# Splitting weights two row chunks at a time, in the memory their float64 words are loaded into

## The chip, the core and the metric

The kernel runs on one core of a Trainium2 chip. The metric is the device time of one execution in microseconds (us). A core has a matrix engine (PE, TensorE), a vector engine (DVE), a scalar engine (ACT), GpSimd (POOL) and a queue engine (SP) that issues this kernel's DMA transfers. Each engine executes its own instructions in program order and waits on semaphores for the others; the on-chip memory has 128 partitions, and the size of an instruction is given by its elements in each partition.

## The reference

Eight batches of 576 tokens go through an attention over 32 packed queries a head and then through a channel mix:

```python
def sm_attn(qq, kk, vv):
    s = scale * np.matmul(qq, kk.transpose(0, 1, 3, 2))
    s = s - np.max(s, axis=-1, keepdims=True)
    a = np.exp(s)
    a = a / (np.sum(a, axis=-1, keepdims=True) + 1e-09)
    return np.matmul(a, vv)
p_packed = sm_attn(p, k, v)
out = sm_attn(q, p_packed, p_packed)
...
x_prev = np.concatenate([np.zeros((B, 1, D), dtype=np.float32), x[:, :-1, :]], axis=1)
xk = mu_k * x + (1.0 - mu_k) * x_prev
xr = mu_r * x + (1.0 - mu_r) * x_prev
k = np.maximum(xk @ w_k, 0.0)
v = k * k @ w_v
r = 1.0 / (1.0 + np.exp(-(xr @ w_r)))
return (r * v).astype(np.float32)
```

q, k, v and p are float32 of 8 batches x 8 heads x 576 (p: 32) x 64; x has 8 x 576 rows of 512. The weights w_r (512 x 512), w_k (512 x 1024) and w_v (1024 x 512) arrive as float64.

## The kernel before

**Blocks.** The 4608 tokens are handled in nine blocks of 512. For each block PE computes the gates (`gates`: xr with w_r, four row tiles of 128 tokens by four chunks of 128 of the sum), the keys (`keys`: xk with w_k, eight column tiles by four chunks) and the values (`values`: the squared keys with w_v, eight chunks by four row tiles). Each product is three matmuls, since both sides are kept as a rounded high part and a low part (`_h` and `_l`): high by high, high by low, low by high. Block 0 lies inside batch 0; block 1 has 64 rows of batch 0 and 448 of batch 1.

**The attention** of a batch runs ahead of the blocks that need it: k is transposed (`transposed_on_pe` for the first two batches, `transposed` on DVE for the rest), `front` makes the scores of the packed queries, the softmax of `weights_of` and the packed values; `back` makes the second scores (line 611), the second softmax on DVE and ACT (lines 635 to 658, in two halves of the batch that interleave) and the output (line 666); `mixed_in` copies it to `xt` (line 688). `mix` then scales and adds (lines 721 on ACT and 725 on DVE), and `split` makes high and low (741 on ACT, 743 on DVE), xr first.

**The weights.** `convert` takes one row chunk of 128 rows and 512 columns at a time: 4 for w_r, 8 for w_k, 8 for w_v, 20 in all. It takes one of four `staged` slots and one of eight `sq` slots, loads the chunk's float64 words as pairs of 32-bit words (512 KB), and when they have landed takes a `tmp` slot for the float32 words m. Line 286 (ACT) makes exponent and high mantissa from the upper words by a scaled copy, lines 288, 290 and 292 (DVE) shift it, set the sign and add the bits of the lower words. Then `sq` and `staged` are given back, line 296 (ACT) rounds m to the high part and line 298 (DVE) subtracts to the low part, both into constant tiles for the whole weight, and the chunk's event is set. `gates` waits for the events of the chunk's w_r, `keys` for w_k, `values` for w_v.

`sq` slots also hold block 0's xr (four, until the gates are done) and the squared keys (eight a block).

**The order** of all engines is made when the program is built, by a planner (`Flow`). Each piece of work is a generator that asks for events, slots or an engine. The planner always takes the piece that could start first by its own clock; where several could start at once, the lower rank goes first. Its costs for an instruction of n elements are in lines 190 to 200, for a load in 205 to 211. A dependent step is ready 0.22 us after the one before it. What it emits is then the fixed order of each engine's queue; the real waits are semaphores. Ranks: batch 0 about 10, the mixing of block 0 11.5, w_r and w_k 13.6 (`RANK_W`), batch 1's loads 14.29, w_v 15.2 (`RANK_V`). The loads of the first two w_r chunks have ranks of their own, `FIRST`, just behind batch 0's loads. Until the gates of block 0 are nearly done, the planner puts small matmuls (`spare`, line 899) where it expects PE to be idle, to keep its clock up; they compute nothing that is used.

Of the kernel before, what the change touches and what calls it, by code (L numbers as in the profile page):

```python
# [8 lines left out]
F32 = mybir.dt.float32  # L9
F32R = mybir.dt.float32r  # L10
U32 = mybir.dt.uint32
AF = mybir.ActivationFunctionType
ALU = mybir.AluOpType
# [150 lines left out]
def attn_pack_channel_mix(ctx: ExitStack, tc: tile.TileContext, q, k, v, p, mu_k, mu_r, w_k, w_v, w_r, out):  # L164
    nc = tc.nc
    B, H, S, D = q.shape
    NP = p.shape[2]
    DM, DF = w_k.shape
    P = 128
# [5 lines left out]
    NC = DM // P  # L175
    NF = DF // P
# [3 lines left out]
    WP = 512  # L180
# [3 lines left out]
    flow = Flow()  # L184


    FIRST = 10.09, 10.29
    RANK_1, RANK_MIX, RANK_W, RANK_V, LOADS_1 = 14.28, 11.5, 13.6, 15.2, 14.29

    def vec(n, after=None):  # L190
        return "vector", 0.07 + 1.04e-3 * n, after, None

    def vec2(n, after=None):
        return "vector", 0.07 + 0.53e-3 * n, after, None

    def act(n, after=None, table=None):
        return "scalar", 0.14 + 0.72e-3 * n, after, table
# [4 lines left out]
    def pe(us, after=None):  # L202
        return "tensor", us, after, None

    def load(dst, src, issue, us):
        yield "queue", issue, None, None
        nc.sync.dma_start(dst, src)  # L207
        begin = max(flow.free.get("dma", 0.0), flow.t + 0.46)
        flow.free["dma"] = begin + us
        flow.free["queue"] = max(flow.free["queue"], begin - 2.0)  # L210
        flow.now.t = begin + us + LANDS
# [6 lines left out]
    def reached():  # L218

        yield None, 0.0, None, None  # L220
# [3 lines left out]
    const = ctx.enter_context(tc.tile_pool(name="const", bufs=1))  # L224
    sb = ctx.enter_context(tc.tile_pool(name="sb", bufs=1))
    ps = ctx.enter_context(tc.tile_pool(name="ps", bufs=1, space=bass.MemoryType.PSUM))
    BUFS = dict(raw=3, kq=4, vt=2, pt=1, a=2, aT=1, pm=2, e=2, a2=1, xt=4, tmp=4, xk=NC, sq=NF, sig=4,
                pa=2, both=1, m=4, staged=4)
    dram = ctx.enter_context(tc.tile_pool(name="dram", bufs=1, space=bass.MemoryType.DRAM))
    for tag, n in BUFS.items():  # L230
        flow.pool(tag, n)
# [2 lines left out]
    def tile_(shape, dtype, tag, slot, name=None):  # L234
        return sb.tile(shape, dtype, name=name or tag, tag=f"{tag}{slot}")
# [22 lines left out]
    ident = const.tile([P, P], F32, name="ident")  # L258
    make_identity(nc, ident)

    wk_h = const.tile([P, NC, DF], F32R, name="wk_h")
    wk_l = const.tile([P, NC, DF], F32R, name="wk_l")
    wr_h = const.tile([P, NC, DM], F32R, name="wr_h")
    wr_l = const.tile([P, NC, DM], F32R, name="wr_l")
    wv_h = const.tile([P, NF, DM], F32R, name="wv_h")
    wv_l = const.tile([P, NF, DM], F32R, name="wv_l")

    def convert(w, hi, lo, c, o, n, event, first=None):

        rank = flow.now.rank  # L270
        if first:
            flow.now.rank = first
        staged = yield from flow.take("staged")
        slot = yield from flow.take("sq")
        st = tile_([P, 2 * WP], U32, "sq", slot, "st")
        yield from load(st[:, :2 * n], w[c * P:(c + 1) * P, o:o + n].bitcast(U32), 0.46, 3.5e-3 * n)
        flow.now.rank = rank
        yield from reached()
        sm = yield from flow.take("tmp")
        m = tile_([P, WP], U32, "tmp", sm, "m")[:, :n]  # L280
        w0, w1 = (st[:, :2 * n].rearrange("p (n two) -> p two n", two=2)[:, j, :] for j in range(2))

        yield act(n)
        nc.scalar.activation(m.bitcast(F32), w1.bitcast(F32), AF.Copy, scale=2.0 ** -112)
        yield vec2(n)
        nc.vector.tensor_scalar(m, m, 3, None, op0=ALU.logical_shift_left)
        yield vec(n, after=0.0)
        nc.vector.scalar_tensor_tensor(m, w1, 0x80000000, m, op0=ALU.bitwise_and, op1=ALU.bitwise_or)  # L290
        yield vec(n, after=0.0)
        nc.vector.scalar_tensor_tensor(m, w0, 29, m, op0=ALU.logical_shift_right, op1=ALU.bitwise_or)
        flow.give("sq", slot)
        flow.give("staged", staged)
        yield act(n)
        nc.scalar.copy(hi[:, c, o:o + n], m.bitcast(F32))
        yield vec(n)
        nc.vector.tensor_tensor(lo[:, c, o:o + n], m.bitcast(F32), hi[:, c, o:o + n].bitcast(F32), op=ALU.subtract)
        flow.give("tmp", sm)
        flow.set(event)  # L300

    ts, vts, pts, xts, xt2 = {}, {}, {}, {}, {}

# [42 lines left out]
    def back_to_issue():  # L346
        flow.now.t = flow.free["queue"]
# [402 lines left out]
    def keys(i):  # L750
        for f in range(NF):
            slot = yield from flow.take("m")
            ph = ps.tile([P, 512], F32, name="ph", tag=f"m{slot}")[:, :TB]
            fs = slice(f * P, (f + 1) * P)
            for c in range(NC):
                yield from flow.wait(("xk", i, c), ("wk", c, f * P // WP * WP))
                yield pe(0.69)
                flow.now.t -= flow.LAG
                _, xh, xl = xks[i, c]
                nc.tensor.matmul(ph, wk_h[:, c, fs], xh, start=(c == 0), stop=False)  # L760
                nc.tensor.matmul(ph, wk_h[:, c, fs], xl, start=False, stop=False)  # L761
                nc.tensor.matmul(ph, wk_l[:, c, fs], xh, start=False, stop=(c == NC - 1))  # L762
                if f == NF - 1:
                    flow.give("xk", xks.pop((i, c))[0])
            flow.spawn(squared(i, f, slot, ph), 0, flow.t + flow.LAG)
# [19 lines left out]
    def gates(i):  # L785
        for t in range(NT):
            slot = yield from flow.take("m")
            pr = ps.tile([P, DM], F32, name="pr", tag=f"m{slot}")
            ts_ = slice(t * P, (t + 1) * P)
            if i == 0 and t == NT - 1:  # L790

                flow.keep_busy = 0.0
                flow.give("m", 3)
            for c in range(NC):
                yield from flow.wait(("xr", i, c), *(("wr", c, o) for o in range(0, DM, WP)))
                yield pe(0.69)
                flow.now.t -= flow.LAG
                _, xh, xl = xrs[i, c]
                nc.tensor.matmul(pr, xh[:, ts_], wr_h[:, c, :], start=(c == 0), stop=False)  # L799
                nc.tensor.matmul(pr, xh[:, ts_], wr_l[:, c, :], start=False, stop=False)  # L800
                nc.tensor.matmul(pr, xl[:, ts_], wr_h[:, c, :], start=False, stop=(c == NC - 1))  # L801
                if t == NT - 1:
                    flow.give("sq", xrs.pop((i, c))[0])
            flow.spawn(gated(i, t, slot, pr), 0, flow.t + flow.LAG)

    def gated(i, t, slot, pr):
        sg = yield from flow.take("sig")
        sig = tile_([P, DM], F32, "sig", sg)
        yield act(DM, table="sigmoid")
        nc.scalar.activation(sig, pr, AF.Sigmoid)  # L810
        flow.give("m", slot)
        sigs[i, t] = sg, sig
        flow.set(("sig", i, t))

    def values(i):
        slots, pv = {}, {}
        for f in range(NF):
            yield from flow.wait(("sq", i, f), *(("wv", f, o) for o in range(0, DM, WP)))
            sf, hl = sqs.pop((i, f))
            for t in range(NT):  # L820
                if f == 0:
                    slots[t] = yield from flow.take("m")
                    pv[t] = ps.tile([P, DM], F32, name="pvo", tag=f"m{slots[t]}")
                ts_ = slice(t * P, (t + 1) * P)
                yield pe(0.69)
                flow.now.t -= flow.LAG
                sh, sl = hl[:, 0, ts_], hl[:, 1, ts_]
                nc.tensor.matmul(pv[t], sh, wv_h[:, f, :], start=(f == 0), stop=False)  # L828
                nc.tensor.matmul(pv[t], sh, wv_l[:, f, :], start=False, stop=False)  # L829
                nc.tensor.matmul(pv[t], sl, wv_h[:, f, :], start=False, stop=(f == NF - 1))  # L830
                if f == NF - 1:
                    flow.spawn(done(i, t, slots[t], pv[t]), 0, flow.t + flow.LAG)
            flow.give("sq", sf)
# [42 lines left out]
        flow.set("mu")  # L876

    def weights():
        first = list(FIRST)
        for c in range(NC):  # L880
            for o in range(0, DM, WP):
                flow.spawn(convert(w_r, wr_h, wr_l, c, o, WP, ("wr", c, o), first.pop(0) if first else None), RANK_W)
        for o in range(0, DF, WP):
            for c in range(NC):
                flow.spawn(convert(w_k, wk_h, wk_l, c, o, WP, ("wk", c, o)), RANK_W)
        for f in range(NF):
            for o in range(0, DM, WP):
                flow.spawn(convert(w_v, wv_h, wv_l, f, o, WP, ("wv", f, o)), RANK_V)

    flow.spawn(all_loads(), 10)  # L890
    flow.spawn(fronts(), 10)
# [36 lines left out]
```

## Time and profile before

| | us |
|---|---|
| median of 3 runs | 599.08 |
| the runs | 602.93, 598.65, 599.08 |
| the profiled execution | 602.04 |
| its span on the core | 600.3 |
| mean granted PE clock (1 is full) | 0.997 |

Two further views are of use. The first is the busy share of each engine in 40 slices of 15 us, in tenths:

```profile
PE   9999999999999999998999999999999999999997
...
DVE  1499999966779769745962977186404812551321
ACT  3578784863585675543833575257524703631410
```

DVE is full from the third slice to the eighth (30 to 120 us), PE nearly everywhere; a slice in which PE computes only fillers reads as busy too. The second is the loads of the weights, issued by SP, with their number, size and the median time from issue to landing:

```profile
st<-in_moe_w_k SPq DMA_DIRECT2D x8, 512.0 KB, 6.2
st<-in_moe_w_v SPq DMA_DIRECT2D x8, 512.0 KB, 5.6
...
st<-in_moe_w_r SPq DMA_DIRECT2D x4, 512.0 KB, 6.7
```

### The profile page before, as it was taken

How to read it: one execution, taken by the hardware profiler on the slowest of the kernel's cores; microseconds unless marked ns; L12 is line 12 of the kernel's file. 1: busy time of each engine (PE TensorE's matmuls, PEld its weight loads, DVE VectorE, ACT ScalarE, POOL GpSimd, SP SyncE). 2: the span in 40 equal slices, each digit the busy share in tenths (PEclk: the TensorE clock that was granted, in tenths of full speed). 3: DMA queues.
4: the chain of work that ended last, by engine and by line, in shares of the span. 5: the costliest groups of instructions: out<-in, count | busy, mean ns of one | idle time of the engine just before them, and what ended most of it. 6: DMA issues, size and time to landing. Idle time of an engine off the chain costs nothing.

```text
span 600.3 us, 10117 instructions
## 1 busy us (share of the span) xinstructions
PE 587.6 (98%) x3924; PEld 465.4 (78%) x3924; DVE 372.3 (62%) x713; ACT 317.4 (53%) x555; POOL 2.1 (0%) x23
## 2 busy tenths in 40 slices
PE   9999999999999999998999999999999999999997
PEld 8777677787777777676777787778788888888886
DVE  1499999966779769745962977186404812551321
ACT  3578784863585675543833575257524703631410
POOL 0000000000000000000000000000000000000000
PEclk9999999999999999998999999999999999999999
DMA  8894661674665760764636343200100010001001
GB/s 194 250 281 120 218 149 42 141 168 84 143 135 130 155 137 15 186 142 70 133 82 166 89 77 93 79 0 1 58 13 1 1 70 1 0 1 70 1 0 71
DMA packets 170895, 56.51 MB, mean 94 GB/s; under 512 B 147808, under 2 KB 162144, under 8 KB 170848
## 3 DMA queue, kind: packets, MB, share of 16 engines
q1 hardware_dynamic: 170848, 55.87, 38.1%
q8 instruction: 31, 0.51, 0.3%
q14 instruction: 16, 0.13, 0.1%
HBM read 42.86 MB, written 12.98 MB: 93 GB/s over the span
## 4 chain that ended last, share of the span: by engine, by line
PE 80%; DVE 6%; SPq 5%; DMA 4%; ACT 2%; issue 2%; ACTq 0%; DVEq 0%
PE pvo L828 11%; PE pvo L830 11%; PE pvo L829 11%; PE ph L760 10%; PE ph L762 9%; PE ph L761 9%; SPq L207 5%; PE pr L799 4%; PE pr L801 4%; PE pr L800 4%; PE pa L666 2%; DVE m L290 2%; PE pa L611 1%; PE pa L478 1%; DMA vt<-in_v 1%
## 5 line engine op out<-in xcount | busy, mean ns | idle before, releaser
L760 PE MATMUL ph<-xk,wk_h 128*128 128x512 f32 x288 | 115.2, 400 | 0.0
L828 PE MATMUL pvo<-wv_h,sq 128*128 128x512 f32 x288 | 114.0, 396 | 0.0
L761 PE MATMUL ph<-xk,wk_h 128*128 128x512 f32 x288 | 112.7, 391 | 0.0
L762 PE MATMUL ph<-xk,wk_l 128*128 128x512 f32 x288 | 112.7, 391 | 0.0
L829 PE MATMUL pvo<-wv_l,sq 128*128 128x512 f32 x288 | 112.2, 390 | 0.0
L830 PE MATMUL pvo<-wv_h,sq 128*128 128x512 f32 x288 | 112.1, 389 | 0.0
L771 ACT ACTIVATE r<-ph 128x512 f32<-128x512 f32 x72 | 43.1, 598 | 93.5 <-PE ph L762 92.4
L778 DVE CAST sq<-r 128x512 fp32r<-128x512 f32 x72 | 30.2, 419 | 92.3 <-ACT r L774 89.9
L828 PEld LDWEIGHTS pvo<-wv_h,sq 128*128 128x128 f32 x288 | 54.0, 188 | 17.2 <-issue 6.3
L760 PEld LDWEIGHTS ph<-xk,wk_h 128*128 128x128 f32 x288 | 54.2, 188 | 16.2 <-issue 5.2
L725 DVE SCALAR_TENSOR_TENSOR x<-xt,mus,x 128x512 f32<-128x512 f32 (+7 forms) x128 | 60.4, 510 | 6.4 <-ACT x L721 6.2
L762 PEld LDWEIGHTS ph<-xk,wk_l 128*128 128x128 f32 x288 | 54.3, 189 | 11.6
L830 PEld LDWEIGHTS pvo<-wv_h,sq 128*128 128x128 f32 x288 | 54.1, 188 | 11.5
L829 PEld LDWEIGHTS pvo<-wv_l,sq 128*128 128x128 f32 x288 | 54.1, 188 | 10.7
L761 PEld LDWEIGHTS ph<-xk,wk_h 128*128 128x128 f32 x288 | 54.3, 188 | 10.3
L721 ACT ACTIVATE x<-xt,mus 128x512 f32<-128x512 f32 (+7 forms) x128 | 61.5, 528 | 1.3 <-DVE xr L743 1.3
L801 PE MATMUL pr<-wr_h,xr 128*128 128x512 f32 x144 | 56.5, 393 | 1.0 <-DVE xr L743 1.0
L799 PE MATMUL pr<-wr_h,xr 128*128 128x512 f32 x144 | 56.8, 395 | 0.0
L800 PE MATMUL pr<-wr_l,xr 128*128 128x512 f32 x144 | 56.1, 390 | 0.0
L810 ACT ACTIVATE sig<-pr 128x512 f32<-128x512 f32 x36 | 21.5, 600 | 60.5 <-PE pr L801 60.4
L780 DVE TENSOR_TENSOR sq<-r,sq 128x512 fp32r<-128x512 f32 x72 | 49.3, 685 | 1.4
L774 ACT ACTIVATE r<-r 128x512 f32<-128x512 f32 x72 | 45.5, 631 | 1.7
(85 smaller groups left out, 681.3 us busy)
## 6 DMA issues: line engine op xcount, KB each, us to landing
out<-sig SPq DMA_DIRECT2D x36, 256.0 KB, 2.5
vt<-in_v SPq DMA_DIRECT2D x16, 512.0 KB, 4.5
raw<-in_k SPq DMA_DIRECT2D x96, 72.0 KB, 2.7
raw<-in_q SPq DMA_DIRECT2D x96, 72.0 KB, 2.8
st<-in_moe_w_k SPq DMA_DIRECT2D x8, 512.0 KB, 6.2
st<-in_moe_w_v SPq DMA_DIRECT2D x8, 512.0 KB, 5.6
far<-at SPq DMA_DIRECT2D x12, 288.0 KB, 2.3
aTd<-far SPq DMA_DIRECT2D x12, 256.0 KB, 2.9
```

The source lines that it names most:

```text
L721: nc.scalar.mul(x32[:, o:o + n], xts[b, c][:, 1 + s:1 + s + n], mus[:, j, c:c + 1])
L725: nc.vector.scalar_tensor_tensor(x32[:, o:o + n], xts[b, c][:, s:s + n], mus[:, j + 1, c:c + 1], x32[:, o:o + n], op0=ALU.mult, op1=ALU.add,)
L760: nc.tensor.matmul(ph, wk_h[:, c, fs], xh, start=(c == 0), stop=False)
L761: nc.tensor.matmul(ph, wk_h[:, c, fs], xl, start=False, stop=False)
L762: nc.tensor.matmul(ph, wk_l[:, c, fs], xh, start=False, stop=(c == NC - 1))
L780: nc.vector.tensor_tensor(hl[:, 1, :], r, hl[:, 0, :].bitcast(F32), op=ALU.subtract)
L799: nc.tensor.matmul(pr, xh[:, ts_], wr_h[:, c, :], start=(c == 0), stop=False)
L800: nc.tensor.matmul(pr, xh[:, ts_], wr_l[:, c, :], start=False, stop=False)
L801: nc.tensor.matmul(pr, xl[:, ts_], wr_h[:, c, :], start=False, stop=(c == NC - 1))
L828: nc.tensor.matmul(pv[t], sh, wv_h[:, f, :], start=(f == 0), stop=False)
L829: nc.tensor.matmul(pv[t], sh, wv_l[:, f, :], start=False, stop=False)
L830: nc.tensor.matmul(pv[t], sl, wv_h[:, f, :], start=False, stop=(f == NF - 1))
```

## The change

`convert` now takes two row chunks at once: two loads of 512 KB into one tile of 1024 float64 words a partition, and each of its six instructions runs over both, 1024 elements. There are ten conversions instead of twenty. The tile lies in memory of its own (one tag for each pair: wr0, wr1, wk0 to wk3, wv0 to wv3), and once m is made, the high and low parts are written to the same place, which has just their size; the constant tiles for whole weights are gone. The staged words no longer take `sq` slots; m takes one, instead of a `tmp` slot. There are three `staged` slots, each for a pair, instead of four for a chunk. Both events of a pair are set when both chunks are done. The third and fourth w_r loads get ranks next to the first two. The matmuls read the same values through `part`.

```diff
-    FIRST = 10.09, 10.29
+    FIRST = 10.09, 10.29, 10.3, 10.31
...
-                pa=2, both=1, m=4, staged=4)
+                pa=2, both=1, m=4, staged=3)
...
-    def convert(w, hi, lo, c, o, n, event, first=None):
-
-        rank = flow.now.rank
-        if first:
-            flow.now.rank = first
+    def convert(name, rows, cols, loads, events, first=()):
+
+        rank, first = flow.now.rank, list(first)
         staged = yield from flow.take("staged")
-        slot = yield from flow.take("sq")
-        st = tile_([P, 2 * WP], U32, "sq", slot, "st")
-        yield from load(st[:, :2 * n], w[c * P:(c + 1) * P, o:o + n].bitcast(U32), 0.46, 3.5e-3 * n)
+        st = const.tile([P, rows, 2 * cols], U32, name="st", tag=name)
+        for dst, src in loads:
+            flow.now.rank = first.pop(0) if first else rank
+            yield from load(dst(st), src.bitcast(U32), 0.46, 3.5e-3 * WP)
+            if dst is not loads[-1][0]:
+                back_to_issue()
         flow.now.rank = rank
         yield from reached()
-        sm = yield from flow.take("tmp")
-        m = tile_([P, WP], U32, "tmp", sm, "m")[:, :n]
-        w0, w1 = (st[:, :2 * n].rearrange("p (n two) -> p two n", two=2)[:, j, :] for j in range(2))
+        sm = yield from flow.take("sq")
+        n = rows * cols
+        m = tile_([P, rows, cols], U32, "sq", sm, "m")
+        w0, w1 = (st.rearrange("p r (n two) -> p two r n", two=2)[:, j] for j in range(2))
...
         nc.vector.scalar_tensor_tensor(m, w0, 29, m, op0=ALU.logical_shift_right, op1=ALU.bitwise_or)
-        flow.give("sq", slot)
         flow.give("staged", staged)
+        w = const.tile([P, rows, 2, cols], F32R, name=name[:2], tag=name)
         yield act(n)
-        nc.scalar.copy(hi[:, c, o:o + n], m.bitcast(F32))
+        nc.scalar.copy(w[:, :, 0, :], m.bitcast(F32))
         yield vec(n)
-        nc.vector.tensor_tensor(lo[:, c, o:o + n], m.bitcast(F32), hi[:, c, o:o + n].bitcast(F32), op=ALU.subtract)
-        flow.give("tmp", sm)
-        flow.set(event)
+        nc.vector.tensor_tensor(w[:, :, 1, :], m.bitcast(F32), w[:, :, 0, :].bitcast(F32), op=ALU.subtract)
+        flow.give("sq", sm)
+        split_w[name] = w
+        for event in events:
+            flow.set(event)
+
+    def part(kind, c, x, cols=slice(None)):
+
+        if kind == "wk":
+            o = cols.start // WP
+            return split_w[f"wk{2 * o + c // 2}"][:, c % 2, x, cols.start - o * WP:cols.stop - o * WP]
+        return split_w[f"{kind}{c // 2}"][:, c % 2, x, cols]
...
     def weights():
-        first = list(FIRST)
-        for c in range(NC):
-            for o in range(0, DM, WP):
-                flow.spawn(convert(w_r, wr_h, wr_l, c, o, WP, ("wr", c, o), first.pop(0) if first else None), RANK_W)
+        def row(j):
+            return lambda st: st[:, j]
+
+        for c in range(0, NC, 2):
+            flow.spawn(convert(
+                f"wr{c // 2}", 2, DM, [(row(x), w_r[(c + x) * P:(c + x + 1) * P, :]) for x in range(2)],
+                [("wr", c, 0), ("wr", c + 1, 0)], FIRST[c:c + 2],
+            ), RANK_W)
```

The spawns of w_k (four pairs of the same 512 columns) and w_v (four pairs) change in the same way, at the same ranks as before, and the matmuls of `gates`, `keys` and `values` take `part(...)` for the slices of the constant tiles.

More of the change, by code (lines that the diff above doesn't have):

```diff
@@ L259, in attn_pack_channel_mix @@
     make_identity(nc, ident)
[L261 to L266, printed above, removed]
-    def convert(w, hi, lo, c, o, n, event, first=None):
-        rank = flow.now.rank
-        if first:
-            flow.now.rank = first
-        staged = yield from flow.take("staged")
-        slot = yield from flow.take("sq")
-        st = tile_([P, 2 * WP], U32, "sq", slot, "st")
-        yield from load(st[:, :2 * n], w[c * P:(c + 1) * P, o:o + n].bitcast(U32), 0.46, 3.5e-3 * n)
+    split_w = {}
+    def convert(name, rows, cols, loads, events, first=()):
+        rank, first = flow.now.rank, list(first)
+        staged = yield from flow.take("staged")
+        st = const.tile([P, rows, 2 * cols], U32, name="st", tag=name)
[4 more added lines that the diff above has]
+                back_to_issue()
         flow.now.rank = rank
         yield from reached()
-        sm = yield from flow.take("tmp")
-        m = tile_([P, WP], U32, "tmp", sm, "m")[:, :n]
-        w0, w1 = (st[:, :2 * n].rearrange("p (n two) -> p two n", two=2)[:, j, :] for j in range(2))
+        sm = yield from flow.take("sq")
+        n = rows * cols
+        m = tile_([P, rows, cols], U32, "sq", sm, "m")
+        w0, w1 = (st.rearrange("p r (n two) -> p two r n", two=2)[:, j] for j in range(2))
         yield act(n)
@@ L759, in keys @@
                 _, xh, xl = xks[i, c]
-                nc.tensor.matmul(ph, wk_h[:, c, fs], xh, start=(c == 0), stop=False)
-                nc.tensor.matmul(ph, wk_h[:, c, fs], xl, start=False, stop=False)
-                nc.tensor.matmul(ph, wk_l[:, c, fs], xh, start=False, stop=(c == NC - 1))
+                nc.tensor.matmul(ph, part("wk", c, 0, fs), xh, start=(c == 0), stop=False)
+                nc.tensor.matmul(ph, part("wk", c, 0, fs), xl, start=False, stop=False)
+                nc.tensor.matmul(ph, part("wk", c, 1, fs), xh, start=False, stop=(c == NC - 1))
                 if f == NF - 1:
@@ L798, in gates @@
                 _, xh, xl = xrs[i, c]
-                nc.tensor.matmul(pr, xh[:, ts_], wr_h[:, c, :], start=(c == 0), stop=False)
-                nc.tensor.matmul(pr, xh[:, ts_], wr_l[:, c, :], start=False, stop=False)
-                nc.tensor.matmul(pr, xl[:, ts_], wr_h[:, c, :], start=False, stop=(c == NC - 1))
+                nc.tensor.matmul(pr, xh[:, ts_], part("wr", c, 0), start=(c == 0), stop=False)
+                nc.tensor.matmul(pr, xh[:, ts_], part("wr", c, 1), start=False, stop=False)
+                nc.tensor.matmul(pr, xl[:, ts_], part("wr", c, 0), start=False, stop=(c == NC - 1))
                 if t == NT - 1:
@@ L827, in values @@
                 sh, sl = hl[:, 0, ts_], hl[:, 1, ts_]
-                nc.tensor.matmul(pv[t], sh, wv_h[:, f, :], start=(f == 0), stop=False)
-                nc.tensor.matmul(pv[t], sh, wv_l[:, f, :], start=False, stop=False)
-                nc.tensor.matmul(pv[t], sl, wv_h[:, f, :], start=False, stop=(f == NF - 1))
+                nc.tensor.matmul(pv[t], sh, part("wv", f, 0), start=(f == 0), stop=False)
+                nc.tensor.matmul(pv[t], sh, part("wv", f, 1), start=False, stop=False)
+                nc.tensor.matmul(pv[t], sl, part("wv", f, 0), start=False, stop=(f == NF - 1))
                 if f == NF - 1:
@@ L878, in weights @@
     def weights():
-        first = list(FIRST)
-        for c in range(NC):
-            for o in range(0, DM, WP):
-                flow.spawn(convert(w_r, wr_h, wr_l, c, o, WP, ("wr", c, o), first.pop(0) if first else None), RANK_W)
-        for o in range(0, DF, WP):
[L884 to L888, printed above, removed]
+        def row(j):
[5 more added lines that the diff above has]
+            ), RANK_W)
+        for o in range(0, DF, WP):
+            for c in range(0, NC, 2):
+                flow.spawn(convert(
+                    f"wk{2 * (o // WP) + c // 2}", 2, WP,
+                    [(row(x), w_k[(c + x) * P:(c + x + 1) * P, o:o + WP]) for x in range(2)],
+                    [("wk", c, o), ("wk", c + 1, o)],
+                ), RANK_W)
+        for f in range(0, NF, 2):
+            flow.spawn(convert(
+                f"wv{f // 2}", 2, DM, [(row(x), w_v[(f + x) * P:(f + x + 1) * P, :]) for x in range(2)],
+                [("wv", f, 0), ("wv", f + 1, 0)],
+            ), RANK_V)
     flow.spawn(all_loads(), 10)
```

## The prediction

> **What bounds the kernel now.** First the page's totals and the chain that ended last, then the fillers' group and stretches of the span.
>
> ```profile
> span 600.3 us, 10117 instructions
> ...
> PE 587.6 (98%) x3924; PEld 465.4 (78%) x3924; DVE 372.3 (62%) x713; ACT 317.4 (53%) x555; POOL 2.1 (0%) x23
> ...
> PE 80%; DVE 6%; SPq 5%; DMA 4%; ACT 2%; issue 2%; ACTq 0%; DVEq 0%
> ...
> L899 PE MATMUL spare<-ident 128*128 128x128 f32 x232 | 32.0, 291 | 1.5 <-POOL ident masks.py:199 1.5
> ...
> 40.00:53.50 13.50, 12.52 (x90) 10.51 (x89) 13.43 (x23) 13.05 (x24) 0.00 (x0) 1.00 0.65 184
> 52.40:596.50 544.10, 540.07 (x3423) 424.11 (x3422) 339.92 (x653) 284.36 (x493) 1.23 (x12) 1.00 0.34 81
> ```
>
> In the rows of stretches the columns behind the length are PE, PEld, DVE, ACT and POOL busy, granted clock, DMA share and GB/s. PE reads 98% busy, but 32.0 us of that are fillers (line 899), which compute nothing. The last two rows split the span in two regimes: from 52.4 us PE idles only 544.10 - 540.07 = 4.0 us, and before it DVE (13.43 of 13.50 us) and ACT (13.05) have no room. So the time is the moment at which PE has its inputs for good, plus a fixed amount of PE work, plus a few gaps. The timeline of PE shows that moment.
>
> ```profile
> 22.76 1.39 PE L611 MATMUL pa<-qT,ppT 64*32 64x288 f32 x32
> ...
> 45.80 0.50 PE L801 MATMUL pr<-wr_h,xr 128*128 128x512 f32 x1 [0.97 <-DVE xr L743]
> ...
> 51.20 0.83 PE L899 MATMUL spare<-ident 128*128 128x128 f32 x6
> 51.78 0.48 PE L799 MATMUL pr<-wr_h,xr 128*128 128x512 f32 x1
> ...
> 60.98 0.39 PE L760 MATMUL ph<-xk,wk_h 128*128 128x512 f32 x1
> ...
> 61.66 0.39 PE L760 MATMUL ph<-xk,wk_h 128*128 128x512 f32 x1
> ...
> 70.01 1.20 PE L444 MATMUL pa<-kT,pt 64*32 64x288 f32 x32 [1.38 <-DVE pt L423]
> ...
> 113.96 0.39 PE L828 MATMUL pvo<-wv_h,sq 128*128 128x512 f32 x1
> ```
>
> The last fillers start at 51.20; then the gates (line 799) run without a break, the keys from 60.98, the values' last row chunk at 113.96. What holds the gates back is DVE, whose timeline (start, duration) goes from its first conversion to the last xr:
>
> ```profile
> 23.17 0.43 DVE L288 TENSOR_SCALAR m<-m 128x512 uint32<-128x512 uint32 x1 [2.50 <-ACT m L286]
> ...
> 24.97 1.44 DVE L635 STREAM_TRANSPOSE e<-pa 128x576 f32<-128x576 f32 x2
> ...
> 31.38 0.69 DVE L290 SCALAR_TENSOR_TENSOR m<-st,m 128x512 uint32<-128x512 uint32 x1
> ...
> 32.18 0.68 DVE L292 SCALAR_TENSOR_TENSOR m<-st,m 128x512 uint32<-128x512 uint32 x1
> ...
> 33.62 0.37 DVE L288 TENSOR_SCALAR m<-m 128x512 uint32<-128x512 uint32 x1
> ...
> 35.22 0.68 DVE L298 TENSOR_TENSOR wr_l<-m,wr_h 128x512 fp32r<-128x512 f32 x1
> 35.82 0.69 DVE L290 SCALAR_TENSOR_TENSOR m<-st,m 128x512 uint32<-128x512 uint32 x1
> 36.42 0.77 DVE L658 STREAM_TRANSPOSE a<-e 128x576 f32<-128x576 f32 x1
> ...
> 40.08 0.42 DVE L288 TENSOR_SCALAR m<-m 128x512 uint32<-128x512 uint32 x1
> 40.53 0.69 DVE L290 SCALAR_TENSOR_TENSOR m<-st,m 128x512 uint32<-128x512 uint32 x1
> 41.26 0.69 DVE L292 SCALAR_TENSOR_TENSOR m<-st,m 128x512 uint32<-128x512 uint32 x1
> 41.87 1.41 DVE L725 SCALAR_TENSOR_TENSOR x<-xt,mus,x 128x512 f32<-128x512 f32 x2
> 43.19 0.68 DVE L298 TENSOR_TENSOR wr_l<-m,wr_h 128x512 fp32r<-128x512 f32 x1
> 43.79 0.68 DVE L298 TENSOR_TENSOR wk_l<-m,wk_h 128x512 fp32r<-128x512 f32 x1
> ...
> 51.72 0.69 DVE L743 TENSOR_TENSOR xr<-x,xr 128x512 fp32r<-128x512 f32 x1
> ```
>
> Three kinds of work share DVE here: conversion (lines 288 to 298), batch 0's second softmax (635 to 658) and the mixing (725, 743). The last xr ends at 51.72 + 0.69 = 52.4. Nothing behind that counts unless PE has to wait for it.
>
> **The change part by part.** (1) Each pair of chunks takes four DVE and two ACT instructions instead of eight and four. No row has these at 1024 elements, so the slope comes from one instruction at two sizes:
>
> ```profile
> L725 DVE SCALAR_TENSOR_TENSOR x<-xt,mus,x 128x512 f32<-128x512 f32 x16 | 11.7, 746 | 0.8 <-ACT x L721 0.8
> ...
> L725 DVE SCALAR_TENSOR_TENSOR x<-xt,mus,x 128x64 f32<-128x64 f32 x16 | 4.4, 273 | 0.6 <-ACT x L721 0.6
> ...
> L721 ACT ACTIVATE x<-xt,mus 128x512 f32<-128x512 f32 x16 | 11.3, 720 | 0.5 <-DVE xr L743 0.5
> ...
> L721 ACT ACTIVATE x<-xt,mus 128x64 f32<-128x64 f32 x16 | 5.4, 340 | 0.0
> ...
> L286 ACT ACTIVATE m<-st 128x512 f32<-128x512 f32 x20 | 13.5, 678 | 4.5 <-DMA st<-in_moe_w_r 3.1 <-DMA st<-in_moe_w_k 0.9 <-ACT m L286 0.6
> ```
>
> DVE: (746 - 273) / 448 = 1.06 ns an element, so 512 more cost 0.54 us. By distances between starts above, a conversion takes 0.45 + 0.73 + 0.61 + 0.60 = 2.39 us (40.08 to 40.53 to 41.26 to 41.87, and 43.19 to 43.79), two of them 4.78. At 1024, three instructions grow by 0.54; the shift (line 288) takes 0.42 where its neighbours take 0.69, so I give it half the slope, 0.27. That is 0.72 + 1.27 + 1.15 + 1.14 = 4.28: a gain of 0.50 a pair, 5.0 over ten pairs. Bounds: nothing, if an instruction of 1024 costs what two cost, and 0.19 x 4 = 0.76 a pair if the whole dependent step's surplus (0.73 - 0.54) falls away. ACT: (720 - 340) / 448 = 0.85 ns an element, so line 286 goes from two of 0.68 to one of 0.68 + 0.43 = 1.11, and line 296 (its cast) likewise: some 0.2 each, 4 us in all, of which little is on the path. The Trainium skill's "Perfetto Trace Analysis", section "Optimizing Scalar/DVE Operations", puts the overhead of a DVE instruction on SBUF at about 60 ns; by it the gain is estimated at 0.24 a pair, and the head below would be some 0.6 us longer than mine. The trace agrees where instructions do not depend on each other (0.60 - 0.54), and shows 0.19 where they do.
>
> (2) The first conversion waits for two row chunks instead of one. Conversion starts at 23.17 now; the second chunk's line 286 follows at about 23.65, and one of 1.11 us ends near 24.8. DVE stands idle there and the softmax takes the place: its scores (line 611) start at 22.76, the first half is done near 23.5, and line 635, which starts at 24.97 behind three conversion instructions, may start near 23.9. So DVE's unbroken work starts 0.7 us later, but the softmax 1.1 us sooner.
>
> (3) The head. From 23.17 to 52.4 DVE works 29.2 us without a hole. The timeline has 21 conversion instructions there, the four w_r chunks, one of w_k and one shift: 5 x 2.39 + 0.35 = 12.3 us; the other 16.9 are softmax and mixing, untouched. After: 23.9 + 16.9 + conversions. Only the two w_r pairs are needed, 8.6 us: 49.4, or -3.0, if no w_k instruction gets in. If as many elements get in as now, with one long instruction more: 2.6 x 4.28 + 1.2 = 12.3, so 53.1, or +0.7. I take 2.6 pairs without the extra, 11.1: 51.9, a gain of 0.5, near the upper end, because DVE still has the wait between 36.42 and 41.87 to fill with conversions.
>
> (4) The stall of 1.38 us at 70.01: PE's order is set by a planner that takes 0.60 us for a vector instruction of 512 (line 191); the dependent ones take 0.73, so DVE runs late and PE finds pt missing. Half as many dependent steps halve that lateness. I take -0.7, between 0 and -1.4.
>
> (5) Loads. Twenty of 512 KB before, twenty after, into memory of their own instead of `sq` slots. w_r's third and fourth go ahead of the two loads of mu, and two of w_k may go ahead of batch 1's k. SP's queue now waits for conversions:
>
> ```profile
> SPq L207 <- DVE m L292: 22.8, 6, 6.9
> ...
> L298 DVE TENSOR_TENSOR wk_l<-m,wk_h x8: 683/684/685, 43.8 to 71.1; 128x512 fp32r<-128x512 f32 x8
> ...
> L298 DVE TENSOR_TENSOR wv_l<-m,wv_h x8: 683/684/691, 78.5 to 109.7; 128x512 fp32r<-128x512 f32 x8
> ```
>
> Those 22.8 us go, and what stands behind them on SP (the w_v loads, batch 1's q, batch 2's k) starts sooner; PE waits for none of it there, so the gain is nothing. Moving mu costs nothing: its first use is the mixing near 40. What covers the k loads is the filler time: pushed out of it, batch 1's transposes would cost PE up to 1.3 us.
>
> (6) A pair is ready only as a whole. The keys start at 60.98 and take 0.68 a chunk (61.66 - 60.98), so they reach the third at 62.3; DVE free of mixing near 53.5 would end two pairs of w_k at 62.1 even if nothing was done before. For the values the last split ends at 109.7 + 0.7 = 110.4, its first need is 113.96, and the pair is wanted one chunk sooner, near 111.2; DVE has saved some 4 us by then. For (5) and (6) together I take +0.3, between 0 and +2. `sq` slots: the intermediate m takes one per pair where each staged chunk took one; no cost, or the wait in (6).
>
> Sum: -0.5 - 0.7 + 0.3 = -0.9 us: 602.0 to 601.1 on the profiled execution (span 600.3 and some 1.7 around it), and 599.1 to 598.2 on the median of the runs shown, which stands 3.0 below the profiled one.
>
> **The rivals.** *A, the head shortens fully*: no w_k gets in (-3.0) and the stall goes (-1.4): 594.7. For it: DVE has no hole from 23.17 on; against: the wait for xt must be filled with something.
>
> *B, slower: long instructions in short holes.* DVE cannot be interrupted. Between steps of the softmax it takes five conversion instructions now (31.38, 32.18, 33.62, 35.22, 35.82). At double length they add 4 x 0.54 + 0.27 = 2.4 us to the chain that ends with line 658 at 36.42; three of line 286, which ACT takes during the mixing, add 3 x 0.43 = 1.3. Less the 1.1 of step (2) that is +2.6, and with the stall kept and one of step (6), +3.6: 602.7. It decides from the point where the holes cost over 1.1. [...]
>
> *C, weights late*: pairs of w_k or w_v miss their slack by several us because DVE favours other work. Every us late is one of PE. Over 6 us would need the w_v pair at 117 instead of 110: 605.5. Against: DVE has less to do than now.
>
> *D, a later stall.* With the order of everything changed, a gap like this one comes or goes (same columns as above):
>
> ```profile
> 270.00:272.00 2.00, 1.08 (x44) 0.67 (x41) 0.00 (x0) 0.38 (x1) 0.00 (x0) 1.00 0.60 128
> 272.00:274.00 2.00, 1.11 (x7) 0.88 (x8) 0.73 (x3) 0.00 (x0) 0.00 (x0) 0.86 0.56 86
> 274.00:276.00 2.00, 2.00 (x14) 1.05 (x20) 0.59 (x1) 0.27 (x1) 0.00 (x0) 0.50 0.74 115
> ```
>
> It idles PE 0.92 + 0.89 us, and the granted clock loses (0.14 + 0.50) x 2 = 1.3: 3.1 in all. One more makes 601.3.
>
> **How the numbers follow.** The forecast (596.3 to 600.3 by itself) has 0.50, A 0.15, B 0.20, C 0.06, D 0.09. The time is 598.2. The range 594.7 to 602.7 holds the forecast, most of A, over half of B and nearly all of D, some 0.8. One per cent, about what a measurement of this kernel can tell from no change, is 6.0 us: under 593.1 lies only A with a gap like D's gone (0.04); over 605.1 C, and B with D (0.07); within, 0.89.
>
> **What would show it.** Right: lines that convert at 1024 elements, ten each, near 0.69 (shift) and 1.23 us on DVE and 1.1 on ACT; DVE's total some 5 us lower; the first softmax transpose before 24.5; the last filler near 50.7; the stall at the batch 1 scores smaller; SP's waits for line 292 gone. Wrong: a last xr after 53 with long conversions between softmax steps (B); PE waiting at the first keys or values for a split (C); new gaps with a lower granted clock after 100 us (D); conversions of 1024 that cost twice those of 512.

## The result, and the profile after

| | before | after |
|---|---|---|
| median (9 runs each) | 598.65 us | 603.59 us |
| range of the runs | 598.06 to 603.64 | 600.97 to 605.49 |
| the profiled execution | 602.04 (span 600.3) | 603.59 (span 601.8) |

The ratio is 1.0069, with a 95% interval of 1.0042 to 1.0097: the change costs about 4 us. It lies inside one per cent, but on the other side of zero from the forecast and 0.9 us beyond its range. Times are medians of all executions, but a ratio leaves out those over 1.5% above the fastest of their kernel: here two of the ten of experiment e2 below (605.09 and 605.67 us, at granted clocks of 0.989 and 0.987).

Three views of the changed kernel: the chain that ended last, the fillers, the stretch behind its last xr. The chain, from the page:

```profile
PE 75%; DVE 12%; SPq 4%; ACT 3%; DMA 3%; issue 2%; DVEq 0%; ACTq 0%
```

The group of the fillers, among the groups by line and form:

```profile
L916 PE MATMUL spare<-ident 128*128 128x128 f32 x268 | 35.7, 288 | 1.5 <-POOL ident masks.py:199 1.5
```

The windows, with the same columns as before:

```profile
55.30:597.70 542.40, 538.82 (x3423) 423.53 (x3422) 333.93 (x620) 280.88 (x479) 1.23 (x12) 1.00 0.33 77
```

DVE's share of the chain that ended last has doubled, from 6% to 12%, and the fillers have grown from 32.0 to 35.7 us: PE waited longer for the head. Behind it, the same 3423 matmuls follow as before. In PE's timeline the places are those shown of before: the second scores, the first key, batch 1's scores; and two later rows.

```profile
23.61 1.20 PE L618 MATMUL pa<-qT,ppT 64*32 64x288 f32 x32
...
63.84 0.39 PE L767 MATMUL ph<-xk,wk 128*128 128x512 f32 x1
...
66.89 1.21 PE L451 MATMUL pa<-kT,pt 64*32 64x288 f32 x32 [0.18 <-DVE pt L430]
...
190.44 1.21 PE L618 MATMUL pa<-qT,ppT 64*32 64x288 f32 x32 [0.91 <-ACT ppT L517]
...
261.92 0.39 PE L767 MATMUL ph<-xk,wk 128*128 128x512 f32 x1
```

The first key is 2.86 us late (63.84 against 60.98). The stall in front of batch 1's scores is 0.18 instead of 1.38, but little of that stays: at block 0's first value (line 835; 95.56 against 93.13) the lag is 2.43. A new stall of 0.91 at 190.44 and one of 0.43 at 227.55 add to it, and by block 3's first key it is 3.9 us (261.92; before, the same matmul starts at 258.04). From there the two executions no longer compare: the one of before lost its clock at 274, as its rows above show, and the one after did not. The lag of 3.9 fits the ratio (0.0069 of 598.65 is 4.1 us); the medians differ by 4.9.

Now DVE from its first work in the head to the last xr. At 1024 elements an instruction is a conversion of w_r or w_k; line 642 is the first step of the second softmax, 665 its last, 732 and 750 the mixing.

```profile
24.43 1.45 DVE L642 STREAM_TRANSPOSE e<-pa 128x576 f32<-128x576 f32 x2 [3.51 <-PE pa L618]
...
28.50 0.69 DVE L286 TENSOR_SCALAR m<-m 128x1024 uint32<-128x1024 uint32 x1
29.21 1.23 DVE L288 SCALAR_TENSOR_TENSOR m<-st,m 128x1024 uint32<-128x1024 uint32 x1
...
31.76 1.22 DVE L290 SCALAR_TENSOR_TENSOR m<-st,m 128x1024 uint32<-128x1024 uint32 x1
...
33.09 0.68 DVE L286 TENSOR_SCALAR m<-m 128x1024 uint32<-128x1024 uint32 x1
...
34.52 1.16 DVE L296 TENSOR_TENSOR wr<-m,wr 128x1024 fp32r<-128x1024 f32 x1
...
36.93 1.21 DVE L288 SCALAR_TENSOR_TENSOR m<-st,m 128x1024 uint32<-128x1024 uint32 x1
38.06 0.77 DVE L665 STREAM_TRANSPOSE a<-e 128x576 f32<-128x576 f32 x1
...
44.59 1.41 DVE L732 SCALAR_TENSOR_TENSOR x<-xt,mus,x 128x512 f32<-128x512 f32 x2
...
54.57 0.69 DVE L750 TENSOR_TENSOR xr<-x,xr 128x512 fp32r<-128x512 f32 x1
```

Before, two conversion instructions stand in the softmax besides the five that the prediction shows:

```profile
29.03 0.68 DVE L298 TENSOR_TENSOR wr_l<-m,wr_h 128x512 fp32r<-128x512 f32 x1
29.63 0.42 DVE L288 TENSOR_SCALAR m<-m 128x512 uint32<-128x512 uint32 x1
```

The softmax starts 0.54 us earlier than before (24.43 against 24.97) and ends 1.64 later (38.83 against 36.42 + 0.77 = 37.19): 14.40 us instead of 12.22. Six conversion instructions lie in it. Durations run into each other by some 0.1, so each is counted from its start to the next start: 0.71 + 1.15 + 1.13 + 0.59 + 1.08 + 1.13 = 5.8 us; the seven short ones of before took 3.6. That is the whole difference: without them the softmax is 8.6 us in both kernels.

The second delay is on ACT. Its timeline, first of the kernel before, where line 688 is the copies to xt, then of the kernel after, where it is 695:

```profile
37.80 0.62 ACT L296 CAST wr_h<-m 128x512 fp32r<-128x512 f32 x1
38.32 0.67 ACT L286 ACTIVATE m<-st 128x512 f32<-128x512 f32 x1
38.90 1.16 ACT L688 COPY xt<-pa 128x576 f32<-128x576 f32 x2
```

```profile
40.02 1.05 ACT L294 CAST wr<-m 128x1024 fp32r<-128x1024 f32 x1 [0.51 <-DVE m L290]
40.99 1.21 ACT L284 ACTIVATE m<-st 128x1024 f32<-128x1024 f32 x1
42.07 1.21 ACT L695 COPY xt<-pa 128x576 f32<-128x576 f32 x2
```

Two conversion instructions stand ahead of the copies in both kernels; after, they are about twice as long, and ACT first waits 0.51 us for a conversion of DVE (line 290). So the lag, 1.64 at the softmax's end, is 3.17 us at the copies (42.07 against 38.90). The mixing then starts on DVE at 44.59 instead of 41.87, and the last xr ends at 55.26 instead of 52.41. One by one, the instructions take what the prediction said (mean ns behind the comma):

```profile
L288 DVE SCALAR_TENSOR_TENSOR m<-st,m 128x1024 uint32<-128x1024 uint32 x10 | 12.3, 1226 | 0.2
...
L284 ACT ACTIVATE m<-st 128x1024 f32<-128x1024 f32 x10 | 11.7, 1171 | 5.0 <-DMA raw<-in_k 2.9 <-DMA st<-in_moe_w_r 2.1
...
L286 DVE TENSOR_SCALAR m<-m 128x1024 uint32<-128x1024 uint32 x10 | 6.8, 681 | 0.0
```

### The profile page after: what moved, and what is told of

Its sections match the earlier page's. It is cut to its first block, busy times and chain, and to the rows that moved or that the text cites. A ratio compares the mean times of both kernels' runs of the same rounds, so it can differ in the third digit from the quotient of the medians.

```text
span 601.8 us, 10113 instructions
## 1 busy us (share of the span) xinstructions
PE 589.3 (98%) x3960; PEld 467.9 (78%) x3960; DVE 368.4 (61%) x673; ACT 315.0 (52%) x535; POOL 2.1 (0%) x23
## 4 chain that ended last, share of the span: by engine, by line
PE 75%; DVE 12%; SPq 4%; ACT 3%; DMA 3%; issue 2%; DVEq 0%; ACTq 0%
PE ph L767 10%; PE ph L768 9%; PE ph L769 9%; PE pvo L835 9%; PE pvo L836 9%; PE pvo L837 9%; PE pr L806 5%; PE pr L808 4%; PE pr L807 4%; SPq L207 4%; DVE x L732 3%; PE pa L673 1%; PE pa L618 1%; DVE m L288 1%; DMA raw<-in_q 1%
## 5 line engine op out<-in xcount | busy, mean ns | idle before, releaser
L767 PE MATMUL ph<-xk,wk 128*128 128x512 f32 x288 | 115.1, 400 | 0.0
L835 PE MATMUL pvo<-wv,sq 128*128 128x512 f32 x288 | 114.0, 396 | 0.0
L768 PE MATMUL ph<-xk,wk 128*128 128x512 f32 x288 | 112.3, 390 | 0.0
L836 PE MATMUL pvo<-wv,sq 128*128 128x512 f32 x288 | 112.2, 390 | 0.0
L769 PE MATMUL ph<-xk,wk 128*128 128x512 f32 x288 | 112.2, 390 | 0.0
L837 PE MATMUL pvo<-wv,sq 128*128 128x512 f32 x288 | 112.1, 389 | 0.0
L835 PEld LDWEIGHTS pvo<-wv,sq 128*128 128x128 f32 x288 | 54.0, 188 | 17.4 <-issue 6.3
L767 PEld LDWEIGHTS ph<-xk,wk 128*128 128x128 f32 x288 | 54.1, 188 | 16.3 <-issue 5.0
L769 PEld LDWEIGHTS ph<-xk,wk 128*128 128x128 f32 x288 | 54.1, 188 | 11.4
L837 PEld LDWEIGHTS pvo<-wv,sq 128*128 128x128 f32 x288 | 54.1, 188 | 11.4
L836 PEld LDWEIGHTS pvo<-wv,sq 128*128 128x128 f32 x288 | 54.1, 188 | 10.6
L768 PEld LDWEIGHTS ph<-xk,wk 128*128 128x128 f32 x288 | 54.1, 188 | 10.2
L806 PE MATMUL pr<-wr,xr 128*128 128x512 f32 x144 | 56.8, 395 | 0.0
L808 PE MATMUL pr<-wr,xr 128*128 128x512 f32 x144 | 56.6, 393 | 0.1
L807 PE MATMUL pr<-wr,xr 128*128 128x512 f32 x144 | 56.1, 390 | 0.0
```

What stands on the lines that cost most here:

```text
L767: nc.tensor.matmul(ph, part("wk", c, 0, fs), xh, start=(c == 0), stop=False)
L768: nc.tensor.matmul(ph, part("wk", c, 0, fs), xl, start=False, stop=False)
L769: nc.tensor.matmul(ph, part("wk", c, 1, fs), xh, start=False, stop=(c == NC - 1))
L806: nc.tensor.matmul(pr, xh[:, ts_], part("wr", c, 0), start=(c == 0), stop=False)
L807: nc.tensor.matmul(pr, xh[:, ts_], part("wr", c, 1), start=False, stop=False)
L808: nc.tensor.matmul(pr, xl[:, ts_], part("wr", c, 0), start=False, stop=(c == NC - 1))
```

## The experiments

Two theories stood. L, length: a conversion instruction that DVE or ACT begins in a short hole of the softmax holds the next step up, and at 1024 elements twice as long. D, loads: w_r's third and fourth load ahead of others make the second scores late, and with them all that follows. The measures are the softmax's length (start of the first of its transposes to the end of the last), the last xr, and the time. The head's rows stand with each experiment; the first is the first transpose, then the last one, then the last xr. Each ratio is to executions of the kernel before measured beside that kernel: their medians are 598.65 us for the changed kernel, 599.29 for e1 to e4 and 599.94 for e5 to e7. The head's rows come from one profiled execution each; those of e6 (607.49 us) and e7 (603.98) lie 2.6 and 3.0 above their kernels' medians.

| kernel | conversion instructions | softmax, us | last xr ends | from softmax to last xr | time, us | ratio to before (95%) |
|---|---|---|---|---|---|---|
| before | 512 | 12.22 | 52.41 | 27.44 | 598.65 | 1 |
| after | 1024 | 14.40 | 55.26 | 30.83 | 603.59 | 1.0042 to 1.0097 |
| e1 | 512 | 12.22 | 50.73 | 27.43 | 612.65 | 1.0103 to 1.0274 |
| e2 | w_r 512, others 1024 | 12.22 | 51.25 | 27.78 | 598.58 | 0.9917 to 0.9991 |
| e3 | 1024 | 14.29 | 57.17 | 30.30 | 610.19 | 1.0079 to 1.0218 |
| e4 | 1024, in long holes only | 10.23 | 46.98 | 24.09 | 599.28 | 0.9961 to 1.0047 |
| e5 | w_r on DVE 512, others 1024 | 12.01 | 51.32 | 28.08 | 597.70 | 0.9935 to 0.9988 |
| e6 | w_r on ACT 512, others 1024 | 13.13 | 57.18 | 31.00 | 604.89 | 1.0058 to 1.0127 |
| e7 | w_r 256, others 1024 | 11.06 | 53.54 | 26.86 | 600.96 | 1.0010 to 1.0069 |

The softmax's length follows the conversions in it. Counted from start to start, they take 3.5, 3.6, 5.6, 3.2, 4.6 and 2.4 us of it in e1, e2, e3, e5, e6 and e7; what is left is 8.6 to 8.8 us in each, as before and after the change.

**e1, halves.** Each of the six steps is cut into pieces of one row chunk; the rest of the change stays. Written so, with whole pairs as pieces, the kernel has the order of the changed one on every engine.

```diff
-        yield act(n)
-        nc.scalar.activation(m.bitcast(F32), w1.bitcast(F32), AF.Copy, scale=2.0 ** -112)
...
+        acts, vecs = grid(512), grid(512)
...
+        for made, pieces in ((scaled, acts), (bits, vecs), (high, acts), (low, vecs)):
+            for j, p in enumerate(pieces):
+                flow.spawn(made(j, p), mine)
```

> The changed kernel with one thing undone: every conversion instruction runs over one row chunk (512 elements) again, two independent strings of six for a pair; loads, memory, slots, early loads and the pair's common event stay as changed. Theory L (length: a conversion instruction of 1024 elements that DVE or ACT begins in a short hole of block 0's softmax and mixing holds the next step up twice as long): the time from the first second-softmax transpose to the end of the last one falls from 14.4 us to 12.2 +- 0.7, the last xr ends at 52 +- 1 instead of 55.3. Rival D (the loads: w_r's third and fourth ahead of the last of q and of mu make the second scores and all behind them late): the chain keeps 14 us or the last xr stays beyond 54.5. The time: 600 +- 2 by L if the later order is as good; a later order with a new gap on PE may hide it, so the last xr decides.

```profile
23.30 0.78 DVE L702 STREAM_TRANSPOSE e<-pa 128x576 f32<-128x576 f32 x1 [2.54 <-PE pa L678]
...
34.75 0.77 DVE L725 STREAM_TRANSPOSE a<-e 128x576 f32<-128x576 f32 x1
...
50.04 0.69 DVE L810 TENSOR_TENSOR xr<-x,xr 128x512 fp32r<-128x512 f32 x1
```

And from its PE timeline:

```profile
124.07 0.80 PE L866 MATMUL pr<-wr,xr 128*128 128x512 f32 x1 [3.66 <-ACT xr L808]
```

The softmax is back to 12.22 us, the length of before, and the last xr (50.73) is earlier than before and than the 51 to 53 expected, with the same loads as the changed kernel: for the head L holds, D does not. The time missed: 612.65. The other order brings a loss of its own at block 1, whose xr comes so late that PE waits 3.66 us at 124.07, 2.08 shortly ahead of that and 4.05 in three more waits behind it. So e1 decides on the head and says nothing on the time.

**e2, only w_r in halves.** Two pairs of ten, those that are converted beside the softmax.

```diff
+    def sizes(name):
+        return (512, 512) if name[:2] == 'wr' else (1024, 1024)
```

> As e1, but only the two w_r pairs are converted in halves; the eight pairs of w_k and w_v stay at 1024 elements. Theory L: the w_r conversions are those that fall between the softmax steps, so nearly all comes back: last xr at 52.5 +- 1, the time 599.5 +- 1.5, faster than the changed kernel by some 3 to 5 us. Rival D: last xr beyond 54.5, time as the changed kernel (603.6).

```profile
23.47 0.78 DVE L706 STREAM_TRANSPOSE e<-pa 128x576 f32<-128x576 f32 x1 [2.54 <-PE pa L682]
...
34.92 0.77 DVE L729 STREAM_TRANSPOSE a<-e 128x576 f32<-128x576 f32 x1
...
50.56 0.69 DVE L814 TENSOR_TENSOR xr<-x,xr 128x512 fp32r<-128x512 f32 x1
```

As L expected (the last xr, 51.25, is 0.25 earlier than its range), and here the time shows it too: 598.58 us, 5.0 under the changed kernel, and 0.1 to 0.8 per cent under the kernel before. The two long pairs of w_r cost all that was lost; a cost of the eight long pairs of w_k and w_v does not show.

**e3, two early loads.** The loads' part undone alone.

```diff
-    FIRST = 10.09, 10.29, 10.3, 10.31
+    FIRST = 10.09, 10.29
```

> The changed kernel with only the first two w_r loads early, as before the change; the third and fourth go behind mu again. Rival D: the waits of PE for raw q shrink from 2.8 us to about 1, the second scores start at 22.8 instead of 23.6, and the last xr is earlier by 0.8 or more than that. Theory L: the chain of the second softmax stays at 14 +- 0.7 us; the last xr gains no more than the 0.8 and stays beyond 54; the time 602 to 605.

```profile
26.87 0.78 DVE L642 STREAM_TRANSPOSE e<-pa 128x576 f32<-128x576 f32 x1 [4.29 <-PE pa L618]
...
40.39 0.77 DVE L665 STREAM_TRANSPOSE a<-e 128x576 f32<-128x576 f32 x1
...
56.48 0.69 DVE L750 TENSOR_TENSOR xr<-x,xr 128x512 fp32r<-128x512 f32 x1
```

```profile
17.29 0.44 PE L401 MATMUL pq<-ident,raw 96*128 96x96 f32 x3 [2.75 <-DMA raw<-in_q]
```

Against D: the scores come later instead of earlier (the last section says why), and the softmax keeps its 14.3 us. The time missed what L expected by 5 us, since block 1 waits for its xr as in e1.

**e4, long holes only.** Instructions as in the changed kernel; the planner puts a conversion back when another step will be ready within 0.5 us, until block 0's last xr.

```diff
         start, ready = self.start(part)
+        if ("xr", 0, 3) not in self.when and part.rank in (13.6, 15.2) and part.want[0] in ("vector", "scalar"):
+            start += 0.5
```

> The changed kernel with 1024 elements an instruction, but until block 0's last xr the planner counts a conversion instruction's start 0.5 us later when it chooses, so that a softmax or mixing step that will be ready within 0.5 us goes first: long conversions only in long holes. Theory L: the second softmax's chain takes 11 +- 1 us, the last xr ends at 49 +- 1.5; the second w_r pair is then the late one (it was done at 42.9 + the cast) and PE may wait for it instead, so PE's unbroken work starts at 51 to 54. Rival D: the chain gets shorter by less than 1 us.

```profile
22.89 1.45 DVE L644 STREAM_TRANSPOSE e<-pa 128x576 f32<-128x576 f32 x2 [2.54 <-PE pa L620]
...
32.34 0.78 DVE L667 STREAM_TRANSPOSE a<-e 128x576 f32<-128x576 f32 x1 [0.24 <-PE pa L675]
...
46.30 0.68 DVE L752 TENSOR_TENSOR xr<-x,xr 128x512 fp32r<-128x512 f32 x1
```

With instructions just as long, but one of them left in the softmax (0.65 us, at 31.44), it takes 10.23 us and the last xr ends 8.3 us earlier than in the changed kernel, 0.5 earlier than expected. So it is not the length alone but a long instruction in a short hole. The last xr is no longer what PE waits for: w_r's two subtractions, put off till then, start at 48.64 and 49.8, PE's gates run unbroken from 49.97, and the first key comes at 61.12 (before, 60.98). The time is that of before.

**e5 and e6, DVE or ACT alone.** As e2, with (1024, 512) and (512, 1024) for w_r's pieces on ACT and DVE.

> As e2 (only w_r's two pairs), but only DVE's four instructions run over one row chunk each; ACT's two stay at 1024 elements. If DVE's long instructions in the softmax's holes are the cause: the softmax chain 12.2 +- 0.5 us as in e2, the last xr 51 to 53, the time within 3 us of e2 (598.6). If ACT's long ones were the larger part (in the changed kernel two of them stand before the second pair of copies to xt, 40.0 to 42.1): the chain falls but the last xr stays beyond 54.

```profile
23.24 1.45 DVE L706 STREAM_TRANSPOSE e<-pa 128x576 f32<-128x576 f32 x2 [2.54 <-PE pa L682]
...
34.48 0.77 DVE L729 STREAM_TRANSPOSE a<-e 128x576 f32<-128x576 f32 x1
...
50.64 0.68 DVE L814 TENSOR_TENSOR xr<-x,xr 128x512 fp32r<-128x512 f32 x1
```

> The counterpart of e5: w_r's two ACT instructions run over one row chunk each, DVE's four stay at 1024. If DVE is the cause: the chain stays at 14 +- 0.5 us and the last xr at 54 to 56, the time near the changed kernel's (603.6 +- 2.5). If ACT is: the last xr comes back to 53 or less.

```profile
26.18 1.45 DVE L706 STREAM_TRANSPOSE e<-pa 128x576 f32<-128x576 f32 x2 [4.43 <-PE pa L682]
...
38.54 0.77 DVE L729 STREAM_TRANSPOSE a<-e 128x576 f32<-128x576 f32 x1
...
56.50 0.68 DVE L814 TENSOR_TENSOR xr<-x,xr 128x512 fp32r<-128x512 f32 x1
```

DVE's halves alone bring everything back. ACT's bring nothing: from the softmax's start to the last xr it is 31.00 us, as in the changed kernel (30.83), though the softmax itself, with five long instructions instead of six, took 13.13, less than expected. The last xr, 57.18, is beyond the 54 to 56 expected, because the scores came later still (first transpose 26.18 against 24.43). As e5 keeps w_r's long ACT instructions and loses no time, they are no cause by themselves; the late copies follow from the order that DVE's long ones led to. That ACT has no share at all isn't shown: in e6 a long one of w_k (1.16 us at 40.15) still stands ahead of the copies.

**e7, quarters.** w_r in pieces of 256.

> As e2, but w_r's instructions run over half a row chunk (256 elements, 16 DVE instructions a pair). If the chain's length follows the size of the piece that gets into a hole (14.4 us at 1024, 12.2 at 512, so some 1.1 us for each 0.27 us of a piece), it falls to 11.2 +- 0.4. But a pair then costs DVE 16 starts instead of 8, some 1 us more, and w_r's second pair is done later: the last xr 49 to 51.5, PE waiting for w_r instead; the time 597 to 601, no better than e2 by more than 1.

```profile
26.68 0.78 DVE L706 STREAM_TRANSPOSE e<-pa 128x576 f32<-128x576 f32 x1 [4.26 <-PE pa L682]
...
36.97 0.77 DVE L729 STREAM_TRANSPOSE a<-e 128x576 f32<-128x576 f32 x1
...
52.86 0.68 DVE L814 TENSOR_TENSOR xr<-x,xr 128x512 fp32r<-128x512 f32 x1
```

The softmax takes 11.06 us, as expected, near the line of the other two sizes (14.40, 12.22); six, seven and eight instructions stand in it at 1024, 512 and 256. The last xr lies beyond the expected 51.5, since the scores were 3 us late in this execution; counted from the softmax's start it is the shortest of the three sizes (26.86). The time is not better than with halves: w_r's last four subtractions start at 54.67, behind the last xr.

## Why the prediction was wrong

The step that failed is (3), the head, and in it the last term of "23.9 + 16.9 + conversions". The sum itself holds, since DVE has no hole there after the change either: 24.4 + 16.9 + 13.9 = 55.3, counted from start to start. The prediction took the conversions at 11.1 us, "as many elements" as before with nothing extra, and at 12.3 at most. In fact 13.9 us of them get in front of the last xr: fourteen instructions of 1024 elements, where 21 of 512 stood before. Six are in the softmax, where they take 5.8 us instead of 3.6; eight are behind it (at 38.76, 39.86, 40.57, 41.71, 42.85, 43.98, 45.91 and 53.44), where they take 8.1 us; eleven short ones took 6.3. Against the 2.2 and 1.8 us stand the softmax's start, 0.54 earlier, and one mixing step less in front of the last xr, 0.6. The estimate of -0.5 became +2.85. A sum of work gives the time of a result only with the right amount of foreign work ahead of it, and that amount was assumed.

The right mechanism stood there as rival B, with 0.20. Its price for the softmax, 2.4 us, is 2.18 measured, though it counted five short instructions doubled where seven gave way to six. On ACT it priced 1.3 for three scaled copies during the mixing; the delay that ACT shows, 1.5, arises ahead of the copies to xt. Its 602.7 missed the time by 0.9, and that is in part luck: step (2) gave 0.54 of the 1.1 that it took off, the stall that it kept fell, the microsecond for a late pair did not come, and it counted no new stall further on. What should have made it the forecast was in the rows that were quoted: every conversion between 31.38 and 36.42 stands between two steps of the softmax.

The Trainium skill ("Perfetto Trace Analysis", "Optimizing Scalar/DVE Operations") says: "If Scalar/Vector aren't saturated, but are causing bubbles on other engines, breaking up instructions may allow work to be completed sooner." Breaking up does that here (e2, 598.58 us, against the changed kernel, 603.59), although the sentence's condition is not met: DVE's timeline shows no idle time between 24.43 and 55.26.

- Step (1) was right in size: 1.23 and 0.68 us on DVE as estimated, 1.17 on ACT instead of 1.11. DVE's total fell from 372.3 to 368.4 us, by 3.9 instead of 5.0. None of it shows in the time; behind the head it is PE that has next to no idle time.
- Step (2) was right in its sign: the softmax goes first. It started at 24.43, not 23.9, since the scores were 0.85 us late in this execution; e1 and e2, with the same loads, have them at 22.5 and 22.6, so the loads aren't the reason.
- Step (4) had the right sign: the stall fell by 1.2, not 0.7. That fewer dependent steps are the reason isn't shown, since batch 1's scores also stand at another place in PE's order, behind four chunks of keys instead of eleven; and the lag at the first value is only 0.4 smaller.
- Steps (5) and (6) cost nothing: the keys follow the gates without a gap at 63.84, and no wait for w_k or w_v appears. But (5) misread mu: its first use is not the mixing near 40, but the small instruction of line 875 within the softmax (at 28.95 before, 28.42 as line 882 after). It waited for nothing in the changed kernel; in e4 DVE stood 0.33 us for mu there.
- Rival D came in a small form, without a lower clock: 0.91 us at 190.44, and a lag of 3.9 at block 3 instead of 2.9 at the first key. Rivals A and C did not come.

What stays open: why single orders (e1, e3) let block 1's xr come so late was seen, not tried. So was the stall at 190.44, which e6 (2.05 us) and e7 (0.79) have too and e2, e4 and e5 have not. And the 0.4% by which e2 and e5 lie under the kernel before is at the edge of what was measured: with all ten executions, e2's median is 0.1% under.

## What to carry to other kernels

Where an engine carries both a chain that something waits for and work that only has to be done some time, the size of the second kind's instructions sets how long each step of the chain may be held up; a longer instruction saves its start and pays where it sits in a hole shorter than itself. So make instructions long where the engine has nothing urgent, and keep them short, or out of short holes, beside the chain. An engine without idle time is not by that a bound on its last result: look at what stands in front of the result, in order.

## What the runs showed of the hardware

PE's granted clock can fall after a pause well under 3 us, and in three profiled executions the head moved with it by about as much as by the change. In e3 PE stood 2.75 us for the first raw q (row above, at 17.29); the granted clock (the column before the last two) is 1.00 up to 18 us, and then:

```profile
18.00:20.00 2.00, 2.00 (x43) 1.64 (x32) 0.00 (x0) 1.54 (x5) 0.00 (x0) 0.76 1.13 235
20.00:22.00 2.00, 2.00 (x46) 1.59 (x44) 0.00 (x0) 0.81 (x3) 0.00 (x0) 0.50 0.89 305
```

At 0.50 the transposes of q take longer (in e6, six take 1.22 us instead of 0.77) and the second scores start at 26.05 instead of 22 to 24. The same happened in e6 (a pause of 1.94 us) and e7 (2.68), and not in the changed kernel (1.99) or e5 (1.70). Further on, a pause of 1.66 us in e2 (up to 223.81) was followed by a clock of 0.50, and one of 2.05 in e6 (up to 193.23) was not. So the length of the one pause doesn't decide it; what does was not tried. The raw q came at a different time in each profiled execution (PE goes on between 16.07 and 17.29), and no filler stands in PE's order at this pause.
